# A planner with new costs and a new table, x blocks at other addresses, and low parts of x and w2 made on VectorE instead of GpSimd in the second feed-forward

## The chip, the cores and the metric

One core of a Trainium2 chip runs one program. The time is device microseconds of one execution. The engines are TensorE (PE, matmuls and transposes; PEld is its weight load), VectorE (DVE), ScalarE (ACT), GpSimd (POOL) and SyncE (SP, which here issues the DMAs). Each engine takes its instructions in the order in which the program has them and waits on semaphores for the others.

## The reference

Three stages, all in float32. The attention is block-causal over 4 batches, 8 heads, 576 positions and 64 columns; the 2304 rows of its result go through two feed-forwards.

```python
scores = np.where(mask, q @ k.T / np.sqrt(D), -1e9)      # mask by blocks of 64
attn = np.exp(scores - scores.max(-1)); attn = attn / (attn.sum(-1) + 1e-09)
x = attn @ v                                             # 2304 x 512
h = x @ w_in                                             # first: 512 -> 1024
solu = h * softmax(h); ln = (solu - mean) / sqrt(var + 1e-06) * g_ln
x = ln @ w_out                                           # 1024 -> 512
h = x @ w2_in                                            # second: 512 -> 2048
out = (h * np.tanh(log1p(exp(h)))) @ w2_out              # 2048 -> 512
```

## The kernel before

Every matmul operand is kept as two fp32r tiles, a high part (ScalarE rounds it) and a low part (what is left over), and a product is three matmuls: high by high, high by low, low by high. The weights arrive as float64; their two 32-bit halves are put together by integer and float operations on VectorE, ScalarE and GpSimd (`weight`, tiles `wraw` and `wem`), and are then split in the same way (`split_weight`).

The attention goes by 16 pairs of heads (`pair`), the first feed-forward by 18 tiles of 128 rows (`moe1_tile`, and `moe1_x2` by 256 rows), and the second by two halves of the 2048 columns, each with five groups of rows (four of 512 and one of 256; `GROUPS`), and in each group four steps of 256 columns (`moe2_pair`). In a group of 512 rows such a step multiplies by Strassen's scheme: seven products of six matmuls with 256 columns each (`prod`), which go in turn into few PSUM banks, with copies on ScalarE and sums on VectorE between them (`copy`, `plus`, tile `xt` in the trace), then the activation, then 24 matmuls of 512 columns (`omm`).

`moe2_x` makes the x blocks of a group: four loads, four differences on VectorE (`diff`, tile `xf`), and seven splits, each a high part on ScalarE (`xbh`) and a low part on GpSimd (`xbl`; for two of the ten blocks the tiles lie in the old `wih` and `wil`). Blocks of both parts stand 528 floats apart.

Nothing of this runs in the order in which it is written. `add` records each step with its engine, a cost, the keys it reads and writes and a priority; `Plan.order` then plays the steps against the costs (`c_dve`, `c_act` and others) and the latencies of the engines (`LAT`, in the order PE, DVE, ACT, POOL, SP), takes on each engine the ready step of the lowest priority, and so fixes the order of every engine and the PSUM bank of every product. The priorities come from the table `PRIO`: a base and a step for each kind of work. A step with `lock` may not run while the planner has one on the other of VectorE and GpSimd.

Of the kernel before, what the change touches and what calls it, by code (L numbers as in the profile page):

```python
# [10 lines left out]
F32 = mybir.dt.float32  # L11
# [15 lines left out]
PRIO = {  # L27
    "load_k": (3584270706, 49.53508582), "load_q": (3584552413, 2.997211538), "load_v": (3584552852, 30.17666404),
# [6 lines left out]
    "w2b": (3584800363, 0.1223531397), "m_x": (3584270481, -7.359126932), "m_h": (3584466166, -2.254093813),  # L35
    "m_v": (3584270377, 9.357429256), "m_w": (3584557870, 6.33404786), "m_u": (3584465474, 5.654352939),
    "m_s": (3584597059, 68.68855867), "m_l": (3584472153, 4.127067276), "m_t": (3584270485, -1.604672924),
    "m_e": (3584598271, 13.20145894), "m_2": (3584466906, 1.251409589), "m_o": (3584597866, 3.694405243),
    "store": (3584271882, 2.346070517), "load_k_b": (3584466375, -0.4078997786),
    "load_q_b": (3584466378, 0.8395418885), "load_v_b": (3584559519, -2.172838748), "tr_b": (3584270603, 85.63069486),  # L40
    "te_b": (3584466669, 21.88305874), "sc_b": (3584464169, 134.7168412), "mx_b": (3584598175, 8.054664166),
    "ex_b": (3584270568, 1.479017813), "su_b": (3584598230, 0.00851345384), "nm_b": (3584552091, 66.60840871),
    "pt_b": (3584270636, -0.9432254557), "pe_b": (3584270488, 0.2673815775), "pv_b": (3584464031, 70.47618497),
    "po_b": (3584269612, 69.4503458), "f_x": (3584558387, 3.529061523), "f_t": (3584466403, -0.8489929687),
    "f_s": (3584552262, 55.84067482), "f_h": (3584559956, 25.46036702), "f_c": (3584270484, -0.9543860343),
    "f_d": (3584269368, 3.538408075), "f_v": (3584464336, 40.97717236), "f_p": (3584465168, 9.220698474),
    "f_q": (3584466866, 0.03331880098), "f_o": (3584589259, 357.8175481), "f_a": (3584465747, 4.127067276),
    "f_e": (3584271879, 2.346070517),
# [18 lines left out]
class Plan:  # L67
# [3 lines left out]
    LAT = (0.21, 0.07, 0.07, 0.1, 2.4, 0.0)  # L71
# [185 lines left out]
def c_dve(n):  # L257
    return (78 + 1.03 * n) / 960.0


def c_act(n, sbuf=False, acc=False, ptr=False):
    return 0.076 + n / 1160.0 + 0.04 * sbuf + 0.18 * acc + 0.09 * ptr


def c_ts(n):
    return (100 + 1.08 * n) / 960.0


def c_tt(n):
    return (110 + 2.3 * n) / 960.0  # L270
# [3 lines left out]
def kernel(  # L274
# [27 lines left out]
    EDGE = 104  # L302
# [92 lines left out]
    def weight(raws, ems, src, tag, idx, paths, after=(), pair=False):  # L395
# [12 lines left out]
        def ex():  # L408
            return em.t[:, 0, 0:wd]
# [13 lines left out]
        add(DVE, (78 + wd / 2) / 960, lambda: nc.vector.tensor_scalar(ex(), hi(), 0x7FF00000, None, op0=ALU.bitwise_and),  # L423
            r=[rk], w=[ek], prio=pri(tag, idx), lock=True)
        add(DVE, (78 + wd / 2) / 960, lambda: nc.vector.tensor_scalar(  # L425
# [43 lines left out]
        else:  # L469
# [12 lines left out]
        add(POOL, c_tt(wd), lambda: nc.gpsimd.tensor_tensor(  # L482
            out=mf(), in0=mf(), in1=ex().bitcast(F32), op=ALU.mult), r=[ek], w=[mk], **pt)
# [93 lines left out]
    def pair(p, xt):  # L577
        b, h2 = divmod(p, HP)

        def pri(tag, i):  # L580
            base, step = PRIO[tag if p < 8 else tag + "_b"]
            return base + step * i
# [85 lines left out]
        def sums(ts):  # L668
            a, n_ = ts
            c = [sm.key(x, t) for x in range(2) for t in range(a, a + n_)]  # L670
            add(DVE, 0.12, lambda: nc.vector.tensor_scalar(
                sm.t[:, :, a:a + n_], sm.t[:, :, a:a + n_], 1e-9, None, op0=ALU.add), w=c, prio=pri("su", p))
            add(DVE, 0.1, lambda: nc.vector.reciprocal(sm.t[:, :, a:a + n_], sm.t[:, :, a:a + n_]), w=c, prio=pri("su", p))  # L673
# [130 lines left out]
    def moe1_tile(i, xts, lth, ltl):  # L804
# [48 lines left out]
        add(DVE, 0.12, lambda: nc.vector.tensor_scalar(c(2), c(2), 1e-9, None, op0=ALU.add), w=[st.key(2)], prio=pri("m_u", i))  # L853
        add(DVE, 0.12, lambda: nc.vector.reciprocal(c(2), c(2)), w=[st.key(2)], prio=pri("m_u", i))
# [3 lines left out]
        add(DVE, 0.12, lambda: nc.vector.tensor_scalar(c(4), c(4), -1.0 / DFF, None, op0=ALU.mult),  # L858
# [4 lines left out]
        add(DVE, 0.12, lambda: nc.vector.tensor_scalar(c(6), c(6), 1.0 / DFF, 1e-6, op0=ALU.mult, op1=ALU.add),  # L863
# [26 lines left out]
    def moe1_x2(g, lth, ltl):  # L890
# [9 lines left out]
        for c2 in range(KD // 2):  # L900
# [3 lines left out]
            for cc in range(2):  # L904
                for k0 in range(0, KF, 4):
                    first = cc == 0 and k0 == 0
                    add(PE, 12 * 0.115, lambda s=s, c=2 * c2 + cc, k0=k0: mm(s, c, k0, k0 + 4),
                        r=[x.key(o) for x in (lth, ltl) for o in range(2)]
                        + [y for kk in range(k0, k0 + 4) for y in hl("wo", kk)],
                        w=[xk] + ([xo.key()] if first else []), acq=[s] if first else None, prio=pri("m_2", 2 * g + 1))  # L910
# [20 lines left out]
    blk_h = Rot(None, "xbh", NBLK, (P, 512 + 16), F32R)  # L931
    blk_l = Rot(None, "xbl", NBLK, (P, 512 + 16), F32R)
# [18 lines left out]
    def open_right():  # L951
        at_cm.__exit__(None, None, None)
        cm = tc.tile_pool(name="m2a", bufs=1, side="right")
        p = cm.__enter__()
        opened["r"] = cm
        for j in range(2):
            slot(p, j)
        xf_r.make(p)
        blk_h.make(p, NRIGHT)
        p.tile([P, 32], F32, name="edge_f")  # L960
        blk_l.make(p, NRIGHT)
        p.tile([P, EDGE], F32, name="edge_g")
        for r in (blk_h, blk_l):
            r.tiles = [t[:, 0:512] for t in r.tiles]

    def open_mid():
        slot(None, 2)
        for r, t in ((blk_h, wih), (blk_l, wil)):
            flat = t.rearrange("p a b -> p (a b)")
            r.tiles += [flat[:, 2912 + 528 * i:3424 + 528 * i] for i in range(2)]  # L970
# [5 lines left out]
    def open_left():  # L976
# [6 lines left out]
        for r in (gh_r, gl_r, blk_h, blk_l, ob_r):  # L983
            r.make(p)
        for r in (blk_h, blk_l):
            r.tiles = [t[:, 0:512] for t in r.tiles]
# [48 lines left out]
    def moe2_pair(cnt, half, g, m, first, last, xs, oslots):  # L1035
# [12 lines left out]
        def prod(k, a, b, s, key, start):  # L1048
# [9 lines left out]
            add(PE, 0.7, go, r=[("w2i", j, c, x) for c in range(2) for x in "hl"] + [xb.key(), xl.key()]  # L1058
# [59 lines left out]
    def moe2_x(cnt, g):  # L1118
# [16 lines left out]
        def split(b, f):  # L1135
# [4 lines left out]
            add(POOL, c_tt(512), lambda: pool_lo(l.t, f.t, h.t), r=[f.key(), h.key(), at_], w=[l.key()],  # L1140
                prio=pri("f_s", cnt + 0.01 * b))
# [136 lines left out]
```

## Time and profile before

| | |
|---|---|
| median of 3 runs | 809.52 us (806.14 to 811.68) |
| the profiled execution | 808.99 us, of which the span from first to last instruction is 807.2 us |
| TensorE busy | 781.4 us, 97% of the span |
| VectorE, ScalarE, GpSimd busy | 516.4, 442.8 and 309.2 us |
| attention with part of the first feed-forward | 0 to about 205 us |
| rest of the first feed-forward | to about 398 us |
| second feed-forward | 398 to 807 us |

The share of busy time is read against the span; what an engine that is busy 97% of it still loses is seen in its waits, in the granted clock, and in the spacing of its matmuls.

### The profile page before, as it was taken

To read this page: it belongs to the slowest core of one execution; us is meant where nothing else is said; L and a number is where in the kernel's file an instruction comes from. 1 tells how busy PE (TensorE), PEld (TensorE's weight loads), DVE (VectorE), ACT (ScalarE), POOL (GpSimd) and SP (SyncE) were. 2 spreads that over 40 slices of the span, in tenths; PEclk is the share of its full clock that TensorE was granted. 3 is DMA by queue.
4 is the path that set the end of the run, shared out by engine and by line. 5 is a ranking of instruction groups with operands and counts; after the bars stand their busy time and mean duration, and the time that the engine had idled before them with its cause. 6 is when DMAs were issued, how large, how long until landed. Compare 5 with 4: busy or idle time off the path is not lost.

```text
span 807.2 us, 14839 instructions
## 1 busy us (share of the span) xinstructions
PE 781.4 (97%) x5700; PEld 692.1 (86%) x5700; DVE 516.4 (64%) x972; ACT 442.8 (55%) x988; POOL 309.2 (38%) x350
## 2 busy tenths in 40 slices
PE   7999998999999999999999899999999999999998
PEld 6877877779888988999998788999888989898886
DVE  6888988899644999333778774234896742532522
ACT  5888978678564654333746445345655634243431
POOL 2378778656433724312324425004153332200300
PEclk9999999999999999999999899999999999999999
DMA  7745471433012233000322433001424250310111
GB/s 154 169 127 138 113 184 43 116 96 119 14 44 66 83 114 105 27 27 28 105 81 90 130 119 105 1 27 53 143 79 157 66 165 19 131 37 18 40 53 53
DMA packets 93159, 69.38 MB, mean 86 GB/s; under 512 B 64160, under 2 KB 77984, under 8 KB 93088
## 3 DMA queue, kind: packets, MB, share of 16 engines
q1 hardware_dynamic: 91824, 68.12, 29.6%
q8 instruction: 45, 0.74, 0.4%
q10 hardware_dynamic: 1264, 0.31, 0.2%
q14 instruction: 26, 0.21, 0.1%
HBM read 54.25 MB, written 14.16 MB: 85 GB/s over the span
## 4 chain that ended last, share of the span: by engine, by line
PE 76%; DVE 14%; ACT 4%; issue 3%; DMA 1%; POOL 1%; SPq 0%; ACTq 0%; DVEq 0%; POOLq 0%
PE ps L1112 22%; PE ps L1055 22%; PE ps L833 10%; PE ps L896 10%; PE ps L749 3%; PE ps L665 3%; PE ps L770 3%; DVE nmx L719 2%; ACT pt L677 2%; PE ps L880 2%; DVE wem L425 1%; DVE wem L423 1%; PE ps L777 1%; DVE xf L1132 1%; DVE ptw L755 1%
## 5 line engine op out<-in xcount | busy, mean ns | idle before, releaser
L1067 DVE TENSOR_TENSOR xt<-ps,xt 128x256 f32<-128x256 f32 x104 | 43.9, 423 | 132.4 <-PE ps L1055 128.7
L733 POOL TENSOR_SCALAR pt<-pt,sm 128x192 f32<-128x192 f32 (+4 forms) x160 | 88.7, 575 | 59.7 <-DVE sm L673 22.6
L328 POOL TENSOR_TENSOR xbl<-xf,xbh 128x512 fp32r<-128x512 f32 x48 | 69.7, 1468 | 87.1 <-ACT xbh L319 68.2
L1055 PE MATMUL ps<-xbh,w2ih 128*128 128x256 f32 x312 | 92.9, 298 | 5.3 <-DVE xt L1067 2.9
L677 ACT ACTIVATE pt<-ps,nmx 128x448 f32<-128x448 f32 (+4 forms) x160 | 82.4, 535 | 25.5 <-DVE nmx L719 16.5
L482 POOL TENSOR_TENSOR wem<-wem 128x512 f32<-128x512 f32 x40 | 56.3, 1409 | 100.0 <-DVE wem L479 66.1
L1063 ACT ACTIVATE xt<-ps 128x256 f32<-128x256 f32 x104 | 39.3, 379 | 98.8 <-PE ps L1055 88.0
L1055 PE MATMUL ps<-xbl,w2ih 128*128 128x256 f32 x312 | 88.4, 283 | 0.0
L1055 PE MATMUL ps<-xbh,w2il 128*128 128x256 f32 x312 | 88.2, 283 | 0.0
L896 PE MATMUL ps<-lth,woh 128*128 128x256 f32 x288 | 81.2, 282 | 0.0
L896 PE MATMUL ps<-lth,wol 128*128 128x256 f32 x288 | 80.7, 280 | 0.0
L896 PE MATMUL ps<-ltl,woh 128*128 128x256 f32 x288 | 80.7, 280 | 0.0
L1055 PEld LDWEIGHTS ps<-xbh,w2ih 128*128 128x128 f32 x312 | 59.5, 191 | 9.6 <-ACT xt L1063 3.6
L1055 PEld LDWEIGHTS ps<-xbl,w2ih 128*128 128x128 f32 x312 | 59.8, 192 | 1.0
L1055 PEld LDWEIGHTS ps<-xbh,w2il 128*128 128x128 f32 x312 | 59.7, 191 | 0.0
L328 POOL TENSOR_TENSOR wil<-xf,wih 128x512 fp32r<-128x512 f32 x12 | 15.8, 1332 | 107.0 <-ACT wih L319 107.0
L896 PEld LDWEIGHTS ps<-lth,wol 128*128 128x128 f32 x288 | 55.0, 191 | 0.0
L896 PEld LDWEIGHTS ps<-lth,woh 128*128 128x128 f32 x288 | 54.1, 188 | 0.7 <-ACT pt L677 0.2
L896 PEld LDWEIGHTS ps<-ltl,woh 128*128 128x128 f32 x288 | 54.1, 188 | 0.3
L749 PE MATMUL ps<-ident,pt 128*128 128x128 f32 x400 | 50.2, 278 | 3.7 <-DVE kl L325 3.5
L749 PEld LDWEIGHTS ps<-ident,pt 128*128 128x128 f32 x400 | 45.6, 144 | 7.1 <-DVE kl L325 3.5
L833 PE MATMUL ps<-wih,xh 128*128 128x512 f32 x144 | 46.6, 405 | 0.2 <-ACT kh L319 0.2
(146 smaller groups left out, 2244.0 us busy)
## 6 DMA issues: line engine op xcount, KB each, us to landing
wraw<-in_moe_w_in_dram SPq DMA_DIRECT2D x24, 512.0 KB, 4.3
wraw<-in_moe_w_out_dram SPq DMA_DIRECT2D x24, 512.0 KB, 3.5
xf<-x_d SPq DMA_DIRECT2D x36, 256.0 KB, 2.9
qraw<-in_q_dram SPq DMA_DIRECT2D x30, 160.0 KB, 3.3
x_d<-xo SPq DMA_DIRECT2D x18, 256.0 KB, 2.3
acc_d<-ob SPq DMA_DIRECT2D x18, 256.0 KB, 2.0
ob<-acc_d SPq DMA_DIRECT2D x18, 256.0 KB, 3.6
out_dram<-ob SPq DMA_DIRECT2D x18, 256.0 KB, 2.0
```

Source lines behind the costliest of these rows:

```text
L328: nc.gpsimd.tensor_tensor(out=dst, in0=src, in1=hi.bitcast(F32), op=ALU.subtract)
L482: add(POOL, c_tt(wd), lambda: nc.gpsimd.tensor_tensor(out=mf(), in0=mf(), in1=ex().bitcast(F32), op=ALU.mult), r=[ek], w=[mk], **pt)
L665: nc.tensor.matmul(out=dst, lhsT=a.t[hs, t * P:(t + 1) * P], rhs=m.t[hs, o + c0:o + c1], start=(i == 0), stop=(i == 2))
L677: add(ACT, c_act(EXT[t], acc=True), lambda: nc.scalar.activation(out=pp.t[:, x * EXT[t]:(x + 1) * EXT[t]] if t < 4 else pp.t[:, x * EXT[t] ...
L733: nc.gpsimd.tensor_scalar(pp, pp, sm.t[:, x, t:t + 1], 1.0, op0=ALU.mult, op1=ALU.mult)
L749: nc.tensor.transpose(ps2(s)[:, a, o:o + P], pts[t].t[:, c * P:(c + 1) * P], ident)
L833: nc.tensor.matmul(out=ps2(hp)[:, hf, :], lhsT=x.t[:, kk, :], rhs=w[:, kk, hf * 512:(hf + 1) * 512], start=bool(first), stop=bool(last))
L896: nc.tensor.matmul(out=ps(s)[:, (c % 2) * 256:(c % 2) * 256 + 256], lhsT=w[:, kk, cs], rhs=x.t[:, kk, :], start=(kk == 0 and i == 0), stop ...
L1055: nc.tensor.matmul(out=ps(s)[:, 0:256], lhsT=sl_i[j, w][:, c, a, :], rhs=x.t[:, mv], start=(start and c == 0 and i == 0), stop=(c == 1 and ...
L1063: add(ACT, c_act(256), lambda: nc.scalar.activation(out=part(x, i), in_=ps(s)[:, 0:256], func=AF.Copy), r=[key] + need, w=[x.key(i)], prio ...
L1067: add(DVE, c_dve(256), lambda: nc.vector.tensor_tensor(out=part(x, i), in0=ps(s)[:, 0:256], in1=part(x, i), op=ALU.add), r=[key], w=[x.key ...
L1112: nc.tensor.matmul(out=ps(oslots[t]), lhsT=x.t[:, tsl], rhs=sl_o[j, wk][:, jj, :], start=(first and jj == 0 and i == 0), stop=(last and jj ...
```

## The change

- The table `PRIO` is another, with tags of their own (`_a`) for the first two pairs of the attention and a tag `f_l` for the low parts of x. The planner's latencies and costs are others: a VectorE or ScalarE result is now taken to be seen after 0.21 and 0.18 us (0.07 each before), and most costs are lower.
- In the second feed-forward the low part of an x block is made on VectorE (60 of them in the program), and so is the last product of a weight of the `w2b` kind, that is of all but the first two of the eight steps' weights (24 products).
- The x blocks lie 512 floats apart, and each now starts 64 bytes below a multiple of 512 bytes, counted from the start of a weight tile; before, that distance went from block to block in steps of 64 bytes. Two dummy tiles of 112 floats and a smaller last one set this.

```diff
-    LAT = (0.21, 0.07, 0.07, 0.1, 2.4, 0.0)
+    LAT = (0.21, 0.21, 0.18, 0.16, 2.4, 0.0)
...
 def c_dve(n):
-    return (78 + 1.03 * n) / 960.0
+    return (64 + 1.02 * n) / 960.0
...
-    "f_s": (3584552262, 55.84067482), "f_h": (3584559956, 25.46036702), "f_c": (3584270484, -0.9543860343),
+    "f_s": (3584456738, -39.48767097), "f_l": (3584456060, 36.7521964), "f_h": (3584463503, 12.97405671),
...
-        add(POOL, c_tt(wd), lambda: nc.gpsimd.tensor_tensor(
-            out=mf(), in0=mf(), in1=ex().bitcast(F32), op=ALU.mult), r=[ek], w=[mk], **pt)
+        if tag == "w2b":
+            add(DVE, c_dve(wd), lambda: nc.vector.tensor_tensor(
+                out=mf(), in0=mf(), in1=ex().bitcast(F32), op=ALU.mult), r=[ek], w=[mk], lock=True, **pt)
+        else:
+            add(POOL, c_tt(wd), lambda: nc.gpsimd.tensor_tensor(
+                out=mf(), in0=mf(), in1=ex().bitcast(F32), op=ALU.mult), r=[ek], w=[mk], **pt)
...
-            base, step = PRIO[tag if p < 8 else tag + "_b"]
+            base, step = PRIO[tag + ("_a" if p < 2 else "" if p < 8 else "_b")]
...
-    blk_h = Rot(None, "xbh", NBLK, (P, 512 + 16), F32R)
-    blk_l = Rot(None, "xbl", NBLK, (P, 512 + 16), F32R)
+    blk_h = Rot(None, "xbh", NBLK, (P, 512), F32R)
+    blk_l = Rot(None, "xbl", NBLK, (P, 512), F32R)
...
-            add(POOL, c_tt(512), lambda: pool_lo(l.t, f.t, h.t), r=[f.key(), h.key(), at_], w=[l.key()],
-                prio=pri("f_s", cnt + 0.01 * b))
+            add(DVE, c_dve(512), lambda: dve_lo(l.t, f.t, h.t), r=[f.key(), h.key(), at_], w=[l.key()],
+                prio=pri("f_l", cnt + 0.01 * b), lock=True)
```

First place, VectorE where the weights of the fifth step are made while the x blocks of the second group are split (`w2il` is the low part of such a weight, `xf` a difference of x blocks, `gl` the low part of an activation, `wem` a weight in the making; L1067 is `plus`). Before:

```order
L325 TENSOR_TENSOR w2il4_4700<-wem0_95,w2ih4_4698 128x896 [waits Activation_49]
L1132 TENSOR_TENSOR xf4_3208<-xf2_3206,xf4_3208 128x512 [waits Pool_49]
L325 TENSOR_TENSOR gl2_4704<-xt0_134,gh2_4702 128x512 [waits Activation_49]
L1132 TENSOR_TENSOR xf1_3205<-xf1_3205,xf4_3208 128x512 [waits DVE_49]
L325 TENSOR_TENSOR gl3_4705<-xt0_134,gh3_4703 128x512
L479 SCALAR_TENSOR_TENSOR wem1_96<-wraw1_94,wem1_96 128x512
L423 TENSOR_SCALAR wem0_95<-wraw0_93 128x512 [waits DMAHW7_49]
L425 TENSOR_SCALAR wem0_95<-wraw0_93 128x512
L467 SCALAR_TENSOR_TENSOR wem0_95<-wraw0_93,wem0_95 128x512 [waits DVE_49]
L1067 TENSOR_TENSOR xt0_134<-ps3_66,xt0_134 128x256 [waits PE_49,Activation_49]
```

The same place on VectorE now:

```order
L330 TENSOR_TENSOR w2il4_4677<-wem0_95,w2ih4_4675 128x896 [waits Activation_49]
L1075 TENSOR_TENSOR xt0_134<-ps3_66,xt0_134 128x256 [waits PE_49,Activation_49]
L330 TENSOR_TENSOR xbl0_3252<-xf3_3243,xbh0_3246 128x512 [waits Activation_49]
L330 TENSOR_TENSOR xbl1_3253<-xf4_3244,xbh1_3247 128x512 [waits Activation_49]
L484 SCALAR_TENSOR_TENSOR wem1_96<-wraw1_94,wem1_96 128x512
L1140 TENSOR_TENSOR xf4_3244<-xf2_3242,xf4_3244 128x512 [waits DVE_49]
L330 TENSOR_TENSOR xbl3_3255<-xf2_3242,xbh3_3249 128x512 [waits PE_49,Activation_49]
L1140 TENSOR_TENSOR xf1_3241<-xf1_3241,xf4_3244 128x512 [waits DVE_49]
L330 TENSOR_TENSOR xbl9_4692<-xf4_3244,xbh9_4690 128x512 [waits Activation_49]
L1075 TENSOR_TENSOR xt0_134<-ps3_66,xt0_134 128x256 [waits PE_49]
```

The low parts `xbl` stand among the other work of VectorE, and a difference no longer waits for GpSimd. GpSimd's last instruction of the program is now one of the first feed-forward; it has none in the second.

Second place, TensorE in the seventh step of the last group, from the end of one product into the next (`ps1_64` and the like are pairs of PSUM banks, and the products of this step take its two banks in turn; L1055 is `prod`, L1112 `omm`). Before:

```order
L1055 MATMUL ps1_64<-xbh8_4706,w2ih1_3200 128x256
L1055 MATMUL ps1_64<-xbl8_4708,w2ih1_3200 128x256
L1055 MATMUL ps1_64<-xbh8_4706,w2il1_3202 128x256
L1055 MATMUL ps1_64<-xbh9_4707,w2ih1_3200 128x256 [waits DVE_49]
L1055 MATMUL ps1_64<-xbl9_4709,w2ih1_3200 128x256
```

The same step now, one product earlier (L1063 is `prod`, L1120 `omm`):

```order
L1063 MATMUL ps0_63<-wih_89,w2il1_3238 128x256
L1120 MATMUL ps1_64<-w2oh0_3233,gh2_4679 128x512
L1120 MATMUL ps1_64<-w2ol0_3235,gh2_4679 128x512
L1120 MATMUL ps1_64<-w2oh0_3233,gl2_4681 128x512 [waits DVE_49]
L1063 MATMUL ps2_65<-wih_89,w2ih1_3236 128x256 [waits DVE_49,Activation_49]
L1063 MATMUL ps2_65<-wil_90,w2ih1_3236 128x256
L1063 MATMUL ps2_65<-wih_89,w2il1_3238 128x256
```

Three matmuls of 512 columns now stand between two products, and the products of a step go to more banks in turn. Counted over the program, 18 steps had all their seven products (42 matmuls) in one run before, and none has now; a product began in the bank of the product before last, with only one product of six matmuls between, 117 times before and begins so 43 times now.

## Rows read from the trace of the kernel before

**Rows 1.** The page, 40 slices of the span: TensorE's granted clock in tenths.

```profile
PEclk9999999999999999999999899999999999999999
```

**Rows 2.** Windows: busy time of each engine, granted clock, DMA; the two outer stages.

```profile
0.00:205.00 205.00, 190.52 (x1787) 160.27 (x1788) 179.65 (x386) 158.59 (x412) 131.69 (x192) 0.98 0.51 125
...
398.00:807.00 409.00, 399.05 (x2476) 358.10 (x2475) 220.18 (x369) 190.18 (x409) 103.89 (x72) 0.99 0.24 78
```

**Rows 3.** Waits of TensorE from 205 us on: sum, times, longest.

```profile
PE ps L1055 <- DVE xt L1067: 3.7, 4, 1.5
PE ps L1055 <- ACT xt L1063: 2.5, 4, 1.9
PE ps L880 <- POOL e L868: 1.2, 2, 1.0
```

**Rows 4.** Timeline, ScalarE around 447 us: start, length, instruction, idle before.

```profile
447.30 0.72 ACT L477 ACTIVATE wem<-wem,edges 128x512 int32<-128x512 int32 x1 [4.24 <-DVE wem L423]
447.93 0.36 ACT L1063 ACTIVATE xt<-ps 128x256 f32<-128x256 f32 x1
```

**Rows 5.** Timeline, VectorE in the same stretch.

```profile
441.10 0.69 DVE L325 TENSOR_TENSOR gl<-xt,gh 128x512 fp32r<-128x512 f32 x1
441.71 0.69 DVE L1132 TENSOR_TENSOR xf<-xf,xf 128x512 f32<-128x512 f32 x1
442.31 1.80 DVE L325 TENSOR_TENSOR gl<-xt,gh 128x512 fp32r<-128x512 f32 x1
...
445.74 1.52 DVE L423 TENSOR_SCALAR wem<-wraw 128x512 int32<-128x512 int32 x1
```

**Rows 6.** Timeline, GpSimd in the same stretch.

```profile
441.70 6.68 POOL L328 TENSOR_TENSOR xbl<-xf,xbh 128x512 fp32r<-128x512 f32 x4 [3.99 <-ACT xbh L319]
```

**Rows 7.** Windows behind that wait; the first busy column is TensorE, then PEclk.

```profile
449.00:451.00 2.00, 0.58 (x4) 0.38 (x3) 2.00 (x3) 0.28 (x1) 0.80 (x1) 0.58 0.26 91
451.00:456.00 5.00, 5.00 (x21) 4.74 (x22) 1.13 (x3) 1.35 (x4) 0.00 (x0) 0.50 0.37 105
```

**Rows 8.** Waits of TensorE, 580 to 610 us.

```profile
PE ps L1055 <- DVE xt L1067: 2.0, 2, 1.5
PE ps L1055 <- ACT xt L1063: 0.2, 1, 0.2
```

**Rows 9.** Groups on VectorE, 560 to 660 us: count, busy, mean ns, idle before.

```profile
L479 DVE SCALAR_TENSOR_TENSOR wem<-wraw,wem 128x512 int32<-128x512 int32 x10 | 9.0, 904 | 0.8 <-ACT wem L477 0.8
...
L325 DVE TENSOR_TENSOR gl<-xt,gh 128x512 fp32r<-128x512 f32 x8 | 8.0, 1020 | 0.9 <-ACT gh L319 0.8
L423 DVE TENSOR_SCALAR wem<-wraw 128x512 int32<-128x512 int32 x10 | 7.3, 729 | 0.1
L325 DVE TENSOR_TENSOR xl<-xt,xh 128x512 fp32r<-128x512 f32 x10 | 6.5, 688 | 6.3 <-ACT xh L319 6.2
L425 DVE TENSOR_SCALAR wem<-wraw 128x512 int32<-128x512 int32 x10 | 6.4, 638 | 0.0
```

**Rows 10.** One group on VectorE, 320 to 400 us.

```profile
L423 DVE TENSOR_SCALAR wem<-wraw 128x512 int32<-128x512 int32 x3 | 1.3, 421 | 0.0
```

**Rows 11.** Groups on GpSimd, 560 to 660 us.

```profile
L328 POOL TENSOR_TENSOR xbl<-xf,xbh 128x512 fp32r<-128x512 f32 x13 | 18.1, 1410 | 18.0 <-ACT xbh L319 18.0
L482 POOL TENSOR_TENSOR wem<-wem 128x512 f32<-128x512 f32 x10 | 14.8, 1483 | 38.3 <-DVE wem L479 22.8 <-DVE wem L467 15.5
```

**Rows 12.** The chain that ended last, from 400 us: start, length, matmuls in a piece.

```profile
403.95 10.88 PE ps L896 x96
...
512.57 2.85 PE ps L1055 x24
...
744.28 5.25 PE ps L1055 x42
```

**Rows 13.** Waits of TensorE, 0 to 205 us, the two longest groups.

```profile
PE ps L640 <- ACT pt L677: 4.0, 5, 1.6
PE ps L749 <- DVE kl L325: 3.5, 7, 0.8
```

More of the change, by code (lines that the diff above doesn't have):

```diff
@@ L39 @@
[L39 to L43, printed above, removed]
@@ L44 @@
[L44 to L48 removed]
+    "load_k_a": (3584451620, 27.82000018), "load_q_a": (3584455205, 4.663779557),
@@ new lines @@
+    "w2b": (3584457222, 19.73532439), "m_x": (3584463514, 0.6741069332), "m_h": (3584457791, 0.1259128113),
+    "m_v": (3584456756, 5.290128661), "m_w": (3584457181, 0.3365750792), "m_u": (3584455965, 1.524414913),
+    "m_s": (3584455223, 16.83847183), "m_l": (3584456330, 12.16871681), "m_t": (3584456370, 15.64709675),
+    "m_e": (3584456484, 87.4189608), "m_2": (3584458069, -7.390700877), "m_o": (3584453850, 7.29521883),
+    "store": (3584456327, 0.3954655404), "load_k_b": (3584457032, 51.61914762),
@@ L257, in c_dve @@
 def c_dve(n):
-    return (78 + 1.03 * n) / 960.0
+    return (64 + 1.02 * n) / 960.0
 def c_act(n, sbuf=False, acc=False, ptr=False):
-    return 0.076 + n / 1160.0 + 0.04 * sbuf + 0.18 * acc + 0.09 * ptr
+    return 0.05 + n / 1170.0 + 0.04 * sbuf + 0.18 * acc + 0.09 * ptr
 def c_ts(n):
-    return (100 + 1.08 * n) / 960.0
+    return (85 + 1.08 * n) / 960.0
 def c_tt(n):
-    return (110 + 2.3 * n) / 960.0
+    return (80 + 2.28 * n) / 960.0
 @with_exitstack
@@ L301 @@
     NBLK = 10
-    EDGE = 104
+    EDGE = 88
     NRIGHT = 6
@@ L958, in open_right @@
         xf_r.make(p)
+        p.tile([P, 112], F32, name="edge_f")
         blk_h.make(p, NRIGHT)
-        p.tile([P, 32], F32, name="edge_f")
         blk_l.make(p, NRIGHT)
         p.tile([P, EDGE], F32, name="edge_g")
-        for r in (blk_h, blk_l):
-            r.tiles = [t[:, 0:512] for t in r.tiles]
     def open_mid():
@@ L969, in open_mid @@
             flat = t.rearrange("p a b -> p (a b)")
-            r.tiles += [flat[:, 2912 + 528 * i:3424 + 528 * i] for i in range(2)]
+            r.tiles += [flat[:, 2928 + 512 * i:3440 + 512 * i] for i in range(2)]
         flat = xt_r.tiles[0].rearrange("p a b -> p (a b)")
@@ L982, in open_left @@
             slot(p, j)
-        for r in (gh_r, gl_r, blk_h, blk_l, ob_r):
+        for r in (gh_r, gl_r, ob_r):
             r.make(p)
+        p.tile([P, 112], F32, name="edge_h")
         for r in (blk_h, blk_l):
-            r.tiles = [t[:, 0:512] for t in r.tiles]
+            r.make(p)
     def slot_gate(j):
@@ L1056, in go @@
                                          start=(start and c == 0 and i == 0), stop=(c == 1 and i == 2), skip_group_check=not start)
-            add(PE, 0.7, go, r=[("w2i", j, c, x) for c in range(2) for x in "hl"] + [xb.key(), xl.key()]
+            add(PE, 0.706, go, r=[("w2i", j, c, x) for c in range(2) for x in "hl"] + [xb.key(), xl.key()]
                 + ([k1] if k else []), w=[key] + (gks if k == 0 else []), acq=[s] if start else None,
```

34 lines of the change are left out of this document (21 added, 13 removed), and 12 rows, old and new, of the table PRIO.

## The prediction

> **What bounds the kernel now.** I read the span by stages first [rows 2]: TensorE is busy 399 of the 409 us of the second feed-forward and 191 of the 205 us of the attention, and its granted clock is 0.99 and 0.98. So TensorE is the bound, no engine beside it matters unless TensorE waits for it, and the question is what TensorE loses. Three kinds of loss show. The first is waits: after 205 us TensorE waits 3.7 us for sums on VectorE (L1067), 2.5 us for copies on ScalarE (L1063) and 1.2 us for GpSimd [rows 3]. The second is the clock: the page has one slice below full speed [rows 1], which the windows put at 449 to 456 us, where the clock fell to 1.2 GHz behind the first of two such waits [rows 7]. The third is spacing, which no list of waits shows: in the chain, 24 matmuls of products take 2.85 us, 0.119 us each, but the 42 of a step that runs all seven products in a row take 5.25 us, 0.125 each [rows 12].
>
> **Why TensorE waited at 446 and 603 us.** At 447 us ScalarE does a weight's exponent (L477) after 4.24 us of idling for VectorE, and only then the copy that TensorE needs [rows 4]. ScalarE takes its work in order, so the copy stood behind the weight. VectorE was late because its operations took 1.80 and 1.52 us there, against 0.69 for the same `gl` a microsecond earlier [rows 5] and 0.42 for L423 in a quiet stretch [rows 10]; exactly then GpSimd ran four low parts in 6.68 us without a pause [rows 6]. The wait at 603 us has the same parts [rows 8].
>
> **The change part by part, against the profiled execution of 808.99 us** (span 807.2, and 1.8 around it; it lies 0.5 under the median).
>
> *Low parts and products off GpSimd.* After the change GpSimd has nothing to do in the second feed-forward, so what stretched VectorE there is gone. VectorE itself: back to back it starts such an operation every 0.61 us (441.10 to 441.71) [rows 5]. Between 560 and 660 us it takes over 13 low parts and 10 products [rows 11], 23 x 0.61 = 14 us, and the few low parts of the blocks in `wih` beside them, about 2 us more. It gets back what it lost [rows 9]: 10 x (904 - 688) ns on L479, 8 x (1020 - 688) on `gl`, 10 x (729 - 421) on L423 and 10 x (638 - 421) on L425, with the unstretched `xl` at 688 ns and L423 at 421 [rows 10]: 2.2 + 2.7 + 3.1 + 2.2 = 10.2 us, more with the lines left out. So VectorE gains about 6 us of work at most in these 100, and does not become the bound by load.
> What comes back to TensorE: around 447 us 1.9 us for ScalarE (the longest of its four) and 1.4 for VectorE, 3.3 us; and the clock. Its two windows [rows 7] have 5.0 us at 0.50 behind the waits, and 0.58 in the two microseconds ahead, where TensorE mostly idled: 2.5 us of work lost, and 0.2 more of the 0.58 us that it was busy there. Waits and clock: 6.0 us. At 580 to 610 us it is 2.0 + 0.2 = 2.2 us [rows 8]. Bounds: 0 if other waits take their place, 8.9 if what is left of the 6.2 us of L1067 and L1063 [rows 3] goes too. I take 8.2.
>
> *New waits.* A sum that TensorE waits for can now stand behind a low part, 0.61 us. Seven come per group, in eight groups. One wait of that length in each group is 4.9 us, none is 0. VectorE idles more than a third of the time in this stage (220 of 409 us busy [rows 2]) and the planner knows the cost, so I take 1.5, between two and three of them.
>
> *Other work between the products.* The seven products of a step use few banks in turn, and a product that begins in the bank of the product before last waits until that one has been copied or summed. With only one product (0.7 us) between, that is not quite done: a row of 42 loses 5.25 - 42 x 0.119 = 0.25 us [rows 12]. Before, 18 steps ran so, 18 x 0.25 = 4.5 us, and shorter rows lose a part of it; now none does, and the tight reuses fall from 117 to 43. Bounds: 0 and 5. I take 4. This comes from the planner's latency of 0.21 us where it had 0.07: it now sees that a result is late and puts output matmuls between.
>
> *x blocks at other addresses.* No row has the new distance for all blocks. The nearest are the products, 0.119 us a matmul, and the output matmuls of the first feed-forward of the same shape, 96 in 10.88 us or 0.113 [rows 12]. If all 1536 product matmuls went to 0.113, that would be 8.4 us less; the other way the far end is the 0.125 of the rows of 42, though those hold waits, 9 us more. I take 0, since blocks of many distances already run in the x24 row at one rate, and keep 3 us either way for the range.
> The Trainium skill, in "SBUF — State Buffer", section "Who interferes with whom", has a rule that speaks against any price here: TensorE never waits for another engine's access, and its two reading ports, for moving data and for weights, are independent. By that rule this term is exactly 0 and the sum stays as it is; by the row of 0.113 it could be up to 8 us lower. No row of this trace tells the two apart, as the first feed-forward's matmuls differ from the products in more than the address.
>
> *The order of the attention.* GpSimd keeps its work there. TensorE loses 14.5 us [rows 2], mostly in two waits that return with each pair [rows 13]: transposes of q and k wait for a bank that an exponential still reads (4.0 us, 5 times), and transposes of the probabilities for a bank that a low part still reads (3.5 us, 7 times). In the steady pairs the new order has the same sequence on TensorE, with other bank numbers, so the same waits are due. I take 0. Bounds: 4 us better (the first group of waits gone) and the rival's 14.5 worse.
>
> **Sum:** 808.99 - 8.2 + 1.5 - 4.0 = 798.3 in an execution like the profiled one, 798.8 against the median, 1.3% less. One per cent, 8.1 us, is about what a measurement of this kernel tells from no change, so faster means below 801.4 and slower above 817.6.
>
> **The rivals.** *VectorE instead of GpSimd.* The waits at 447 and 603 us move rather than go: five groups on VectorE alone fill 37 of the 100 us from 560 to 660 [rows 9], and its queue now has low parts, weights and sums in one line. For it: TensorE's longest list of waits already names VectorE [rows 3]. Against it: VectorE gets about as much time back as it takes on. Then 8.2 us come back as other waits and only the spacing is won: 808.99 - 4 + 0.5 = 805.5, no change.
> *The port in the first feed-forward.* Six blocks of the first group lie outside `wih`, and their low parts are made while GpSimd still works for the first feed-forward. A low part on VectorE with both inputs in SBUF then runs against GpSimd's operations, at 1.80 instead of 0.69 us [rows 5], and TensorE already waits there for GpSimd's `e` (1.2 us [rows 3]). Six times 1.1 us is 6.6; with half of it in front of TensorE, 3.3 us, so 802.1. For it: the stretch is in the rows. Against it: TensorE has whole 10.88 us pieces of other matmuls to run meanwhile [rows 12].
> The same skill page, same section, gives this as a rule: such a VectorE operation and a GpSimd operation that reads SBUF exclude each other, and whichever is issued second waits it out. The trace agrees in the length of the rows.
> *Slower: the attention's new order.* VectorE is 88% and ScalarE 77% busy there [rows 2], so little slack covers a step that is put behind another. The mechanism is the one of rows 13, a bank that is given back later: TensorE's transposes wait for it in each of 16 pairs, now 14.5/16 = 0.9 us a pair. If that doubles, 14.5 us are lost, and with two more falls of the clock like that of rows 7 (2.7 us each) 19.9: 798.8 + 19.9 = 818.7. It decides from 1.2 us more a pair. For it: every priority and cost in this stage is new. Against it: the sequence on TensorE is the same.
>
> **How the numbers follow.** The forecast 0.60, VectorE instead of GpSimd 0.25, the port 0.07, slower 0.08. The forecast's own bounds (new waits 0 to 4.9, spacing 0 to 5, addresses 3 either way, attention up to 4 better) reach from some 790 to 806; the range is 790.5 to 808, which takes in the first two rivals and leaves out the slower one and a better end than all bounds together. Faster by over 1%: 0.62, with the best part of the second rival; within 1%: 0.30; slower: 0.08.
>
> **What would show it.** In the new profile: no GpSimd row after about 400 us; `gl`, L479 and L423 (by their new lines) at their quiet means of 0.69 and 0.42; no granted clock below 0.9 between 440 and 460 us; waits of TensorE after 205 us at 3 us or less in all; steps without pieces of 42 matmuls, and a step's 42 products and 24 output matmuls together nearer 10.5 than the 10.7 us of now; TensorE busy about 190 us of the attention as before. I am wrong if TensorE's waits name VectorE for 6 us or more, if the attention is longer or shorter by over 4 us, or if the 256-column matmuls step by other than 0.118 to 0.120 us.

## The result and the profile after

The changed kernel takes 788.9 us (median of 4, 788.0 to 790.2) beside 808.8 of the kernel before: ratio 0.9754, 95% interval 0.9717 to 0.9791. That is 20 us less, nearly twice the 10.7 of the forecast's sum, and under the lower end of its range by 1.6 us. The profiled execution has a span of 787.2 us beside 807.2 [rows 2].

By stages, with the windows as in [rows 2], and two more where the kernel before had its stalls (columns: TensorE, its weight loads, VectorE, ScalarE, GpSimd, granted clock, DMA share, GB/s):

```profile
0.00:205.00 205.00, 189.61 (x1774) 158.38 (x1775) 176.78 (x382) 157.41 (x409) 132.57 (x186) 0.98 0.52 125
...
398.00:787.00 389.00, 384.98 (x2465) 349.86 (x2463) 225.26 (x439) 192.42 (x407) 0.00 (x0) 1.00 0.26 81
...
440.00:460.00 20.00, 20.00 (x132) 18.26 (x131) 19.50 (x43) 14.95 (x32) 0.00 (x0) 1.00 0.57 169
580.00:610.00 30.00, 30.00 (x189) 26.92 (x189) 28.55 (x57) 20.70 (x43) 0.00 (x0) 1.00 0.55 176
```

In the attention TensorE idles 15.4 us beside 14.5. Most of the time went from the second feed-forward. TensorE does not idle at 440 to 460 and 580 to 610 us, where the prediction put its loss at 6.0 and 2.2 us [rows 7, 8], the clock there is full, and GpSimd has nothing to do.

TensorE's waits from 205 us on are down to one line, where there were three with 7.4 us [rows 3]:

```profile
PE ps L1063 <- ACT xt L1071: 0.5, 1, 0.5
```

The groups on VectorE, 560 to 660 us, against [rows 9]:

```profile
L330 DVE TENSOR_TENSOR xbl<-xf,xbh 128x512 fp32r<-128x512 f32 x12 | 7.9, 685 | 1.7 <-ACT xbh L324 1.7
L484 DVE SCALAR_TENSOR_TENSOR wem<-wraw,wem 128x512 int32<-128x512 int32 x10 | 6.9, 686 | 0.2 <-ACT wem L482 0.2
L488 DVE TENSOR_TENSOR wem<-wem 128x512 f32<-128x512 f32 x10 | 6.8, 685 | 0.0
...
L330 DVE TENSOR_TENSOR gl<-xt,gh 128x512 fp32r<-128x512 f32 x10 | 6.7, 689 | 1.9 <-ACT gh L324 1.8
...
L430 DVE TENSOR_SCALAR wem<-wraw 128x512 int32<-128x512 int32 x9 | 3.8, 419 | 0.0
L428 DVE TENSOR_SCALAR wem<-wraw 128x512 int32<-128x512 int32 x8 | 3.4, 419 | 0.0
```

Every operation shown is at its quiet length, that of a stretch without GpSimd: `gl` 689 ns instead of 1020, L484 686 instead of 904 (as L479), L428 and L430 419 instead of 729 and 638. VectorE has taken on 22 operations here, the first and third line, and none of its lines is stretched any more.

The chain that ended last around 510 us (start, length, matmuls in a piece):

```profile
503.23 2.83 PE ps L1063 x24
506.06 2.72 PE ps L1120 x12
...
516.44 2.81 PE ps L1063 x24
519.25 0.69 PE ps L1120 x3
519.95 1.41 PE ps L1063 x12
521.36 0.68 PE ps L1120 x3
522.04 0.71 PE ps L1063 x6
522.75 4.08 PE ps L1120 x18
```

From 516.44 on it is one whole step: its 42 product matmuls take 2.81 + 1.41 + 0.71 = 4.93 us, where the row of 42 took 5.25 [rows 12]. And one sign says that something else happened too: 24 product matmuls take 2.83 or 2.81 us and no longer 2.85, that is 0.117 to 0.118 us from one start to the next (called a step of the matmuls below), at or just under the 0.118 to 0.120 that the prediction allowed.

### The profile page after: what moved, and what is told of

Its sections match the earlier page's. It is cut to its first block, busy times and chain, and to the rows that moved or that the text cites. A ratio compares the mean times of both kernels' runs of the same rounds, so it can differ in the third digit from the quotient of the medians.

```text
span 787.2 us, 14801 instructions
## 1 busy us (share of the span) xinstructions
PE 767.6 (98%) x5700; PEld 683.8 (87%) x5700; DVE 523.6 (67%) x1056; ACT 448.0 (57%) x988; POOL 195.4 (25%) x266
## 4 chain that ended last, share of the span: by engine, by line
PE 85%; DVE 9%; ACT 3%; issue 1%; DMA 1%; SPq 0%; DVEq 0%; ACTq 0%
PE ps L1120 25%; PE ps L1063 23%; PE ps L905 13%; PE ps L842 11%; PE ps L674 4%; PE ps L758 3%; PE ps L779 3%; DVE nmx L728 2%; PE ps L889 2%; ACT pt L686 2%; PE ps L786 1%; PE ps L649 1%; DVE kl L330 1%; DVE ql L660 1%; DVE ptw L764 1%
## 5 line engine op out<-in xcount | busy, mean ns | idle before, releaser
L742 POOL TENSOR_SCALAR pt<-pt,sm 128x448 f32<-128x448 f32 (+4 forms) x160 | 92.6, 599 | 48.0 <-DVE sm L682 16.4
L1063 PE MATMUL ps<-xbh,w2ih 128*128 128x256 f32 x312 | 88.8, 285 | 0.5 <-ACT xt L1071 0.5
L1063 PE MATMUL ps<-xbl,w2ih 128*128 128x256 f32 x312 | 87.4, 280 | 0.0
L1063 PE MATMUL ps<-xbh,w2il 128*128 128x256 f32 x312 | 87.3, 280 | 0.0
L905 PE MATMUL ps<-lth,woh 128*128 128x256 f32 x288 | 81.3, 282 | 0.0
L905 PE MATMUL ps<-lth,wol 128*128 128x256 f32 x288 | 80.8, 280 | 0.0
L905 PE MATMUL ps<-ltl,woh 128*128 128x256 f32 x288 | 80.7, 280 | 0.0
L1063 PEld LDWEIGHTS ps<-xbh,w2ih 128*128 128x128 f32 x312 | 58.6, 188 | 3.0 <-ACT xt L1071 0.8
L1063 PEld LDWEIGHTS ps<-xbl,w2ih 128*128 128x128 f32 x312 | 58.7, 188 | 2.1
L1063 PEld LDWEIGHTS ps<-xbh,w2il 128*128 128x128 f32 x312 | 59.5, 191 | 0.0
L905 PEld LDWEIGHTS ps<-lth,wol 128*128 128x128 f32 x288 | 55.1, 191 | 0.0
L905 PEld LDWEIGHTS ps<-lth,woh 128*128 128x128 f32 x288 | 54.1, 188 | 0.9 <-issue 0.5
L905 PEld LDWEIGHTS ps<-ltl,woh 128*128 128x128 f32 x288 | 54.1, 188 | 0.3
L758 PEld LDWEIGHTS ps<-ident,pt 128*128 128x128 f32 x400 | 44.0, 141 | 8.6 <-DVE kl L330 2.4
L842 PE MATMUL ps<-wil,xh 128*128 128x512 f32 x144 | 44.6, 391 | 0.0
L842 PE MATMUL ps<-wih,xl 128*128 128x512 f32 x144 | 44.5, 390 | 0.0
L1120 PE MATMUL ps<-w2oh,xh 128*128 128x512 f32 x108 | 42.1, 390 | 0.0
```

The source lines that it names most:

```text
L742: nc.gpsimd.tensor_scalar(pp, pp, sm.t[:, x, t:t + 1], 1.0, op0=ALU.mult, op1=ALU.mult)
L758: nc.tensor.transpose(ps2(s)[:, a, o:o + P], pts[t].t[:, c * P:(c + 1) * P], ident)
L842: nc.tensor.matmul(out=ps2(hp)[:, hf, :], lhsT=x.t[:, kk, :], rhs=w[:, kk, hf * 512:(hf + 1) * 512], start=bool(first), stop=bool(last))
L905: nc.tensor.matmul(out=ps(s)[:, (c % 2) * 256:(c % 2) * 256 + 256], lhsT=w[:, kk, cs], rhs=x.t[:, kk, :], start=(kk == 0 and i == 0), stop ...
L1063: nc.tensor.matmul(out=ps(s)[:, 0:256], lhsT=sl_i[j, w][:, c, a, :], rhs=x.t[:, mv], start=(start and c == 0 and i == 0), stop=(c == 1 and ...
L1120: nc.tensor.matmul(out=ps(oslots[t]), lhsT=x.t[:, tsl], rhs=sl_o[j, wk][:, jj, :], start=(first and jj == 0 and i == 0), stop=(last and jj ...
```

## The experiments

Theory 1 is that of the prediction, with the sizes that the traces now give: GpSimd's low parts stretched VectorE and so made the waits and the half clock (some 9.5 us), the order took away late banks between products (some 5), and the address moves only the quiet step, the usual time from one matmul to the next where nothing is late. Rival 1: the address made the longer steps between products too. Rival 2: the new order alone made the room, and the engine does not matter.

Three kinds of time are read from each trace. "Second feed-forward" is the stretch from the last transpose of the first feed-forward (L889, L880 in the kernel before) to the end of the span; in the changed kernel it starts at 396.2 us, by the matmul row of that line in the timeline:

```profile
L889 PE MATMUL ps<-ident,e x4: 272/273/273, 395.8 to 396.2; 128*128 128x128 f32 x4
```

so 787.2 - 396.2 = 391.0 us; before it is 807.2 - 398.8 = 408.4. "Double steps" are products whose second matmul starts over 60 ns later than usual, counted from the starts of all matmuls of the trace (55 before, a few of them in the half clock; 9 after). The ratio is to the kernel before on the same chip, whose median was 808.7 to 809.2 us. The two columns in us behind the median and the double steps are each from one profiled execution; the two of the changed kernel differ by 1.4 and 0.5 us.

| kernel | ratio, 95% | median us | up to it | second feed-forward | double steps |
|---|---|---|---|---|---|
| before | 1 | 808.8 | 398.8 | 408.4 | 55 |
| before, addresses alone | 0.9996 (0.9981-1.0011) | 808.2 | 400.9 | 407.8 | 62 |
| before, VectorE alone | 0.9889 (0.9866-0.9912) | 799.4 | 398.5 | 398.2 | 45 |
| before, VectorE, new latencies | 0.9942 (0.9924-0.9961) | 804.2 | 408.4 | 394.3 | 6 |
| after, old addresses | 0.9787 (0.9765-0.9808) | 792.0 | 396.4 | 393.9 | 6 |
| after | 0.9754 (0.9717-0.9791) | 788.9 | 396.2 | 391.0 | 9 |
| after, again | 0.9766 (0.9738-0.9793) | 790.2 | 397.6 | 391.5 | 7 |
| after, GpSimd | 0.9958 (0.9942-0.9974) | 805.8 | 397.3 | 407.0 | 26 |
| after, product alone on GpSimd | 0.9800 (0.9780-0.9820) | 792.9 | 396.8 | 394.6 | 19 |
| after, old latencies | 1.0196 (1.0169-1.0222) | 824.3 | 422.8 | 399.9 | 56 |
| after, distance 0 | 0.9814 (0.9788-0.9839) | 794.2 | 395.3 | 395.3 | 6 |
| after, 128 below | 0.9808 (0.9786-0.9829) | 793.8 | 394.8 | 395.5 | 6 |
| after, 64 above | 0.9798 (0.9778-0.9818) | 792.5 | 396.9 | 393.7 | 6 |
| after, rows split | 0.9730 (0.9706-0.9754) | 787.6 | 395.6 | 391.2 | 8 |

**VectorE alone, in the order of before.** The plan is that of before; only the engine that gets the instruction differs.

```diff
-            add(POOL, c_tt(512), lambda: pool_lo(l.t, f.t, h.t), ...
+            add(POOL, c_tt(512), lambda: dve_lo(l.t, f.t, h.t), ...
-        add(POOL, c_tt(wd), lambda: nc.gpsimd.tensor_tensor(
+        add(POOL, c_tt(wd), lambda: (nc.vector if tag == "w2b" else nc.gpsimd).tensor_tensor(
```

> The kernel before with the low parts of the x blocks and the last product of the second weights done on VectorE, at the places in the plan where GpSimd did them: TensorE's and ScalarE's order is that of before. Theory 1: the stall at 446 to 456 us and the one at 603 us go, 799 to 802 us; granted clock above 0.9 throughout after 205 us; the spacing of the products as before. Rival 2 (VectorE takes GpSimd's place as the engine that is late, and only the new order made room for it): 808 or more, with TensorE waiting for VectorE's sums and low parts. Rival 1 says the same as theory 1 here.

Measured 799.4 us, the second feed-forward 10.2 us shorter. TensorE's waits there fall from 6.2 us [rows 3] to 0.4 (the first line below lies in the first feed-forward), and 440 to 460 us runs at full clock:

```profile
PE ps L880 <- POOL e L868: 2.5, 2, 1.5
PE ps L1055 <- DVE xt L1067: 0.2, 1, 0.2
PE ps L1055 <- ACT xt L1063: 0.2, 1, 0.2
```

```profile
440.00:460.00 20.00, 20.00 (x129) 18.26 (x128) 16.51 (x33) 12.53 (x26) 0.00 (x0) 1.00 0.49 159
```

So the engine alone took the stall away, without any room made by the new order: rival 2 falls. The rows of 42 product matmuls stayed:

```profile
505.25 2.85 PE ps L1055 x24
508.10 2.76 PE ps L1112 x12
510.85 5.26 PE ps L1055 x42
```

Where the 0.25 us of such a row goes is seen in the timeline of this kernel, in three engines at the start of a product (746.22) that waits for VectorE's sum out of its bank:

```profile
745.74 0.42 DVE L1067 TENSOR_TENSOR xt<-ps,xt 128x256 f32<-128x256 f32 x1 [2.81 <-PE ps L1055]
...
745.98 0.19 PEld L1055 LDWEIGHTS ps<-xbh,w2il 128*128 128x128 f32 x1
746.22 0.19 PEld L1055 LDWEIGHTS ps<-wih,w2ih 128*128 128x128 f32 x1
746.32 0.19 PEld L1055 LDWEIGHTS ps<-wil,w2ih 128*128 128x128 f32 x1
...
746.09 0.28 PE L1055 MATMUL ps<-xbh,w2il 128*128 128x256 f32 x1
746.22 0.39 PE L1055 MATMUL ps<-wih,w2ih 128*128 128x256 f32 x1
746.44 0.28 PE L1055 MATMUL ps<-wil,w2ih 128*128 128x256 f32 x1
```

The sum ends at 746.16. A weight load elsewhere starts one matmul ahead of its own (745.98 for the matmul of 746.09); this one starts with its matmul, and the next matmul comes 0.22 us later and not 0.12. TensorE never idles, so no list of waits shows it; it costs 0.106 us, twice in nearly every row of 42. It is no single case: in 43 of the 45 double steps of this kernel the load starts 1 or 2 ns ahead of its matmul, where 117 ns is usual, and a sum or a copy out of a bank ended 50 to 60 ns ahead of the product, which is so in only 2 of the products with a quiet step. In 61 more products the load starts 60 to 100 ns ahead and the step is 134 to 155 ns; from the start of the load to the second matmul it is 225 ns in both groups. So 0.106 us is the full price, and a bank that is less late costs less. The Trainium skill, in "TensorE: Matmul & The Clock Gate", section "LDWEIGHTS (loading the stationary operand)", has a formula that gives an estimate of 128/1.2 = 107 ns for a load of 128 columns. The excess of 106 ns agrees with it; the load's own row, 0.19 us, does not show it, so that the double step is one load in the open is read from the starts.

**GpSimd, in the order of after.** The counterpart, both operations back, with the plan of after:

```diff
-            add(DVE, c_dve(wd), lambda: nc.vector.tensor_tensor(
+            add(DVE, c_dve(wd), lambda: nc.gpsimd.tensor_tensor(
-            add(DVE, c_dve(512), lambda: dve_lo(l.t, f.t, h.t), ...
+            add(DVE, c_dve(512), lambda: pool_lo(l.t, f.t, h.t), ...
```

> The changed kernel with the low parts and the last product of the second weights back on GpSimd, at the places in the plan where VectorE did them: TensorE's and ScalarE's order is that of the changed kernel. Theory 1: VectorE is stretched again (gl near 1.0 instead of 0.69 us), GpSimd's 1.4 us low parts come late, and TensorE waits: 796 to 800 us, with at least one fall of the granted clock after 205 us. Rival 2 (the order alone did it): 789 to 791 us, VectorE stretched but TensorE not waiting. Rival 1: as theory 1.

Measured 805.8 us, 16.0 us more in the second feed-forward, with `gl` at 999 ns and waits of 10.5 us, more than before had:

```profile
PE ps L1063 <- ACT xt L1071: 5.4, 7, 3.2
PE ps L1063 <- DVE xt L1075: 3.4, 4, 1.0
PE ps L1120 <- DVE gl L330: 1.7, 1, 1.7
```

```profile
L330 DVE TENSOR_TENSOR gl<-xt,gh 128x512 fp32r<-128x512 f32 x32 | 31.3, 999 | 11.9 <-ACT gh L324 11.9
L1140 DVE TENSOR_TENSOR xf<-xf,xf 128x512 f32<-128x512 f32 x26 | 29.7, 1141 | 18.4 <-POOL xbl L333 11.1 <-POOL wil L333 4.8 <-DMA xf<-x_d 2.3
```

The granted clock is 0.91 between 440 and 460 us. This order, planned for VectorE, has next to no value with GpSimd in the stage (407.0 beside 407.8 us at the same addresses), only on top of the move; an order planned with the new costs and GpSimd there was not run. The last line shows a second way in which GpSimd holds VectorE up: beside stretching it, VectorE idles 15.9 us ahead of its differences until GpSimd's low parts are done.

**Only the last product of the weights back on GpSimd.** The first of the two edits above by itself.

> The changed kernel with the last product of the second weights alone back on GpSimd; the low parts stay on VectorE, the order of TensorE and ScalarE is that of the changed kernel. With both back the second feed-forward took 16 us more (407.0 against 391.0). If any GpSimd operation beside VectorE's stretches it alike: ten of 1.5 us in 100 us against thirteen low parts and ten products, so about 40 per cent, 5 to 7 us more. If it is the low parts that TensorE waits for and not the stretch: 0 to 2 us more.

Measured 3.6 us more in the second feed-forward than after, between the two: ten double steps more and waits of 2.3 us. So the product is not free on GpSimd, and the low parts, put back on top of it, carry the greater part, some 12 of the 16 us. VectorE is stretched less here than with both back, `xl` most:

```profile
L330 DVE TENSOR_TENSOR xl<-xt,xh 128x512 fp32r<-128x512 f32 x32 | 26.9, 854 | 12.0 <-ACT xh L324 12.0
L330 DVE TENSOR_TENSOR gl<-xt,gh 128x512 fp32r<-128x512 f32 x32 | 21.9, 705 | 9.6 <-ACT gh L324 9.5
```

Over the lines for low parts, differences and weights that adds some 10 us to VectorE's work, and some 35 with both back, for 3.6 and 16.0 us of time. That fits the stretch as the cause, but the low parts alone on GpSimd were not run, and how the 16 us divide between the stretch and VectorE's waits for GpSimd's low parts is not shown.

**Addresses alone, in the kernel before**, and **old addresses in the changed kernel**. Same instructions and order in each pair; the edit is that of the change's tile lines (`EDGE`, the blocks of 528 or 512 elements, the offsets in `wih` and `wil`), made or undone.

> The kernel before with the new addresses of the x blocks alone: the same instructions in the same order on every engine. Theory 1 (the low parts on GpSimd made the waits and the half clock, some 9.5 us; the order took away the bank waits between products, some 5 us; the address is worth the few ns a matmul that are left): 806 to 809 us, the stall at 446 to 456 us stays, and the single longer steps between products (147, 223 ns) stay. Rival 1 (the address makes the longer steps between products, not the order): 801 to 802 us, with the stall still there but the longer steps gone. Rival 2 (the order alone did it all): 808.8 and an unchanged spacing.

> The changed kernel with the x blocks back at the addresses of before: the same instructions in the same order. Theory 1: 789 to 792 us, products stepping at 118 to 119 instead of 117 ns. Rival 1 (the address makes the longer steps): 794 to 797 us, with steps of 147 to 223 ns where a product begins. Rival 2: 789, unchanged spacing.

In the kernel before the address gave nothing that can be told from no change (ratio 0.9996; its interval leaves room for 1.5 us at most). In the changed kernel undoing it costs 2.4 to 2.9 us of the second feed-forward. The intervals of the two ratios, 0.9754 and 0.9787, overlap; what tells the two kernels apart is the spacing of some 2200 matmuls in each trace. Rival 1 falls: the double steps stayed in the one (62) and stayed away in the other (6). What the address moves is the quiet step. With the old addresses the chain of the changed kernel has, for the same pieces as above:

```profile
504.17 2.85 PE ps L1064 x24
507.02 2.76 PE ps L1121 x12
```

that is 0.02 us more per 24 product matmuls and 0.04 more per 12 output matmuls. Over all quiet steps of the stage, those less than 12 ns above the usual, the new addresses lower the mean by 1.2 ns a product matmul and 1.1 ns an output matmul, and 1390 x 1.2 + 763 x 1.1 ns = 2.5 us. In the kernel before the quiet steps fell alike (by 1.3 and 0.8 ns, some 2.4 us), but its profiled execution had some 1.4 us more of waits and double steps. That waits take back there what the steps win is argued from this one trace, not shown.

**Other common distances.** All blocks at distance 0, 128 bytes below and 64 above the weights' place; the first as a diff:

```diff
-        p.tile([P, 112], F32, name="edge_f")
+        p.tile([P, 128], F32, name="edge_f")
-            r.tiles += [flat[:, 2928 + 512 * i:3440 + 512 * i] for i in range(2)]
+            r.tiles += [flat[:, 2944 + 512 * i:3456 + 512 * i] for i in range(2)]
```

> The changed kernel with all x blocks 64 bytes further on, so that each block lies at the weights' own place in 512 bytes (distance 0) and not 64 bytes below it; same instructions, same order. If what counts is that all blocks lie alike: as the changed kernel, 789, the quiet steps of the products at 117 ns. If the distance of 64 bytes below counts: 2 to 3 us more, as with the addresses of before, steps at 118 to 119 ns.

> The changed kernel as it is, again, beside the others of this chip. Both theories: 787 to 791 us, a ratio of 0.973 to 0.978 to before.

> The changed kernel with all x blocks 64 bytes lower, 128 bytes below the weights' place in 512 bytes; same instructions, same order. So far the second feed-forward took 391.0 and 391.5 us at 64 below, 393.9 with the mixed distances of before and 395.3 at distance 0. If 64 below is one good place among the mixed ones, some other distance must be as good as or better than the mean of 393.9: 391 to 393.9 here. If any common distance but 64 below is as bad as 0: 395.

> The changed kernel with all x blocks 64 bytes above the weights' place in 512 bytes; same instructions, same order. If the sign of the distance counts: 393 to 396 us for the second feed-forward (391.0 at 64 below). If only the distance from 0 counts: 391.

Distance 0 takes 395.3 us, 128 below 395.5, 64 above 393.7, the mixture 393.9, 64 below 391.0 to 391.5. So not that all blocks lie alike counts, but where: distance 0 is worse than the mixture, and the sign of the distance counts. At 0 the pieces are

```profile
503.37 2.87 PE ps L1063 x24
506.24 2.75 PE ps L1120 x12
```

at 128 below the pieces of 24 take 2.88 us, and at 64 above the product matmuls are quick and the output matmuls not:

```profile
504.56 2.83 PE ps L1063 x24
507.39 2.76 PE ps L1120 x12
```

The output matmuls read no x block, and what they read lies where it lay in all four. Why they follow the blocks' address is open.

**The planner's latencies.** In the changed kernel back to the old, with everything else new; and, in the other direction, the new ones in the kernel before with VectorE.

```diff
-    LAT = (0.21, 0.21, 0.18, 0.16, 2.4, 0.0)
+    LAT = (0.21, 0.07, 0.07, 0.1, 2.4, 0.0)
```

> The changed kernel, planned with the latencies of before (0.07, 0.07, 0.1 us for VectorE, ScalarE, GpSimd instead of 0.21, 0.18, 0.16), everything else as changed. The plan then has 111 products that begin in the bank of the product before last, where it had 44, and 16 rows of 42 products, where it had none. Theory 1 (each such product finds its bank not yet free, its weights are loaded late and in the open, 106 ns each): 40 to 50 more double steps of 223 ns in the second feed-forward, 4 to 5 us more than the changed kernel: 793 to 795 us. Rival (the waits come from VectorE's and ScalarE's load, the new priorities removed them): 788 to 791 us, double steps as few as in the changed kernel (some 9).

> The kernel before with the low parts and the last product on VectorE as in the run of that alone (799.4 us), planned with the new latencies; priorities, costs and addresses as before. The plan has 46 tight products instead of 124 and no row of 42. Theory 1: the double steps (47 in that run) fall to 10 or fewer and 4 to 6 us go: 793 to 796 us. Rival: the double steps stay, as priorities and costs removed them, 798 to 801 us.

The expectations count the products that begin in the bank of the product before last in another way than the 117 and 43 given with the change; by that count the plan with the old latencies has 104 and the other 43. In the second feed-forward the double steps do what theory 1 says: 56 with the old latencies instead of 9, and 6 with the new ones instead of 45. At 0.106 us each that is 5.0 us more and 4.1 less. The second is what was measured, 3.9 us less (398.2 to 394.3). The first is not all: the stage takes 8.9 us more, beyond the 4 to 5 expected, as some 2 us lie in products that start late and TensorE's waits grow from 0.5 to 1.4 us. With the old latencies the rows of 42 are back:

```profile
501.65 5.27 PE ps L1063 x42
```

Neither whole time came out as expected, since the latencies plan the other stages too: the stretch ahead grew by 9.9 us with the new latencies in the kernel before, and by 26.6 with the old ones in the changed kernel, where a single wait in the attention takes 11.9 us:

```profile
PE ps L758 <- POOL pt L742: 12.1, 2, 11.9
```

In both directions a table of priorities was worse under latencies other than its own.

**How a row begins.** The output rows of the first feed-forward (L905, 96 matmuls of 256 columns) step at 117.8 ns behind a matmul of 512 columns and at 113.3 in a few places, for example in the row at 400.5 us, which follows a product. Their second matmul is made as two of 128 columns:

```diff
+                    step = 128 if c == 0 and kk == 0 and i == 1 else 256
+                    for h in range(0, 256, step):
```

> The changed kernel with the second matmul of each of the nine groups' output rows of the first feed-forward made as two of 128 columns. These rows of 96 step at 117.8 ns behind a matmul of 512 columns, and at 113.3 where they follow a short stall. If the step depends on how the row begins, the longer beginning turns the nine rows to 113 ns: 9 x (96 x 4.5 - 110) ns = 2.9 us less. If it depends on the data or addresses: 9 x 0.1 = 1 us more.

The first row below is the changed kernel's, the second fence this kernel's, the same row of the plan with one matmul more:

```profile
266.79 11.31 PE ps L905 x96
```

```profile
268.16 11.02 PE ps L907 x97
```

The rows turned to the quicker step, 0.29 us each in the six that run in one piece behind a matmul of 512 columns, and the stretch from the first transpose of L889 to the last is 254.9 us, 1.8 shorter than the 256.7 of the changed kernel and its repeat. That is less than the 2.9 expected for nine rows: the others are in pieces, or were quick already. Nor does a late beginning alone do it: in the changed kernel the piece at 194.0 us, whose second matmul comes 90 ns late, steps at 113 ns, and the one at 172.3, with 84 ns, at 118. The median, 787.6 us, is the lowest of all; the interval of its ratio overlaps that of after, so by the trace it is quicker, by the timing alone not yet shown.

## Why the prediction was wrong

The mechanisms in the sum were there and in the direction forecast. The steps that failed are its sizes: 3.5 us too little for GpSimd's work off, and nothing for two terms that brought 2.9 and 2.6 us; the spacing was sized rightly. Against the four terms, in the order of the kernels that isolate them:

- **Low parts and products off GpSimd (-8.2) and new waits (+1.5): -6.7 net, measured -10.2** (before to VectorE alone). This is the largest miss, 3.5 us. The waits went but for 0.4 us and the half clock completely, beyond the 8.2 and the bound of 8.9, and no new waits came in place of the 1.5. The bound left out that the move also brings banks back earlier: ten double steps fewer, up to 1.1 us. The step on VectorE's queue argued from 0.61 us a low part, standing in front of a sum; with its operations at their quiet length VectorE had the sums ready early enough. That the stretch, and not GpSimd's lateness, was what TensorE paid for is likely from the run with the product alone, not shown. Rival "VectorE instead of GpSimd" is refuted, as its 8.2 us stayed away. The Trainium skill has in "SBUF — State Buffer", section "Who interferes with whom", the rule that a VectorE operation with two inputs in SBUF and a GpSimd operation that reads SBUF exclude each other. The traces agree in both directions: `gl` 999 ns with GpSimd in the stage, 689 without.
- **Other work between the products (-4): measured -4.3** (VectorE alone to after with old addresses), or -3.9 by the latencies alone. Size and cause are right, with a correction: what a tight bank costs is the weight load behind it, up to 0.106 us, and TensorE does not idle for it; 39 double steps fewer are 4.1 us.
- **x blocks at other addresses (0): measured -2.4 to -2.9.** This is the step whose reason failed. It argued that blocks of many distances already ran at one rate in the x24 row, so that the address had no price. That one rate is a mixture: its 2.85 us lies between the 2.83 and 2.88 that common distances give. Its other end, 0.113 us a matmul [rows 12], was no effect of addresses either; the split rows show that the same matmuls at the same addresses go from 0.118 to 0.115 us a step over a row with its beginning. The Trainium skill, in the same section of "SBUF — State Buffer", says that TensorE never waits on another engine and reads moving data and weights through independent ports. That is a rule on engines that meet; it does not speak of where an operand lies, and to read a price of exactly 0 out of it was the prediction's own step. The measurement decides: the address of the moving data alone is worth up to 4.5 us (395.5 to 391.0).
- **Everything up to the second feed-forward (0): measured -2.6** in the profiled execution, -1.2 in the repeat. 1.2 us is the wait for GpSimd's `e` [rows 3], which the sum left standing and the new order does not have. The attention did not get faster by its waits: its two longest groups [rows 13] are 1.7 and 3.2 us now, but new ones make up the rest, and TensorE idles 0.9 us more there. What else is in the 2.6 may in part be chance: the granted clock at 10 to 20 and 20 to 30 us was 0.83 and 0.83 before, 0.83 and 1.00 after, 0.71 and 0.78 in the repeat, and the 1.4 us between the two executions of the changed kernel arise ahead of the first transpose of L889, at 139.5 and 140.9 us. In the order of before, with the low parts on VectorE, the wait for `e` grew to 2.5 us, with the longest `e` 2.27 us instead of 1.64: the rival "the port in the first feed-forward", at 1.3 of its 3.3 us, and only in that order.

Together -10.2 - 4.3 - 2.9 - 2.6 = -20.0, the difference of the spans. The terms interact: on top of GpSimd's low parts, the order is worth 0.8 us and the address 0.6 (by the second feed-forward), so both were worth little until the move was made.

The range had a slip too. Its bounds were said to reach down to some 790, with a better end than all of them together left out; but 808.99 - 8.2 - 5 - 3 - 4 = 788.8, and by its own bounds the measured 788.9 was possible.

What stays open: why the step depends on the address, why the output matmuls follow it, and which beginning turns a row to the quicker step.

## What to carry to other kernels

Where TensorE waits for one engine that is slow only while another works, try giving the other's work to the first and look at the sum of both, not at the load of one. A matmul that gets its bank late cost up to a weight load here though TensorE never idled: look at the starts of weight loads, and put other matmuls between. And an address can be a cost like any other: when a kernel is bound by equal matmuls, try some distances between moving data and weights, and size the term from runs, not from rows that mix the distances.

## What was not expected of the hardware

- 64 bytes in the address of the moving data change the step of 256-column products by some 2 ns, and that of 512-column output matmuls, which don't read that data, by as much (means of the quiet steps: 116.8 and 227.1 ns at 64 below, 119.0 and 229.3 at distance 0).
- The same 96 matmuls of 256 columns run at 117.8 ns each, or at 113 when the second of the row is made as two of 128 columns, and keep to it to the end of the row.
- A bank given back too late for the early weight load costs up to 106 ns in the second matmul of the product, while the first starts only some 18 ns late (median of the 45 with VectorE alone).
